# Expert and gate logits of an attention + mixture-of-experts + MLP kernel, computed token by token instead of head pair by head pair

## The chip, the cores and the metric

The kernel runs on one core of a Trainium2 chip. The metric is the device time of one execution in microseconds (us); less is better. Engines are named as the profile names them: PE (TensorE matmul), PEld (TensorE weight load, which overlaps PE), DVE (VectorE), ACT (ScalarE), POOL (GpSimd), SP (SyncE, here only a DMA queue).

## What is computed

Three stages follow each other. Causal attention with a decay for 4 batches of 8 heads of 576 positions and 64 dimensions; a mixture of experts in which each of the 2304 tokens goes to the one expert of 8 with the largest logit; and a dense MLP with a rational activation.

```python
x = attn(q, k, v, f)                      # (4*576 tokens, 8 heads * 64 = 512)
logits = x @ w_gate                       # (2304, 8)
e_idx = argmax(logits, axis=1)
gate_w = softmax(logits)[token, e_idx]
eom = sigmoid(x @ w_output_gate)          # (2304, 8)
for e in range(8):                        # only the rows with e_idx == e
    out[mask] = gate_w * eom[:, e] * (relu(x[mask] @ w1[e]) @ w2[e])
h = out @ w_in
out = P(h) / Q(h) @ w_out
```

The change is in how `x @ w_gate` and `x @ w_output_gate` are made (16 numbers per token in all), and in the short stretch between attention and experts.

## The kernel before, in words

**Attention.** The 32 heads of all batches are worked off as 16 pairs, four pairs to a batch. A pair makes scores on PE (L456, L457, L467, L468, into one of 3 PSUM banks `s`), takes the row minimum on DVE (L479, L491), exponentials on ACT (L511, L522), transposes of the weights on PE (L578, L582, L598, into one of 3 PSUM banks `pt`), copies of these to `pT` on ACT or DVE (L291, L293), and the product with the values on PE (L621, into one of 2 banks `po`). The result of a pair is copied to `ot` (L291 or L293): head dimensions of the two heads on the 128 partitions, the 576 tokens along the row. It isn't yet divided by the softmax's sum.

**The order.** Every step is an `Op` with a wished time and a length for each engine that may do it. `Plan.order` places them greedily on the engines by these numbers and writes each engine's program in that order; engines then work strictly in order, so one that waits holds back all that is behind it. The lengths are the planner's own; the wished times are a table (`T_STEP`, `T_TRANS` and so on).

**A batch.** When a batch's four pairs have `ot`, `batch` adds these steps, in two parts of the tokens (rows 2 to 4 with the 64-row rest first, then rows 0 and 1; a row is 128 tokens). The sums of the two half rows are added (L679), swapped over partitions by a small matmul (L683) and inverted (L697, L698). The logits: for each of the four pairs a matmul with the small weights `wl` (128 partitions, 32 columns: 16 for either head) as the stationary operand and `ot` as the moving one, each pair to its own 32 partitions of one bank `s` (L706); ACT copies the bank to `lgs` (L712); PE transposes `lgs` to token-major, 128 tokens to a matmul, into a bank `pt` (L720); DVE multiplies by the inverted sums (L727) and adds up the 8 heads (L731). Then `choose` (L748 on) picks the expert, `gates_a`, `gates_x` (two exponentials on ACT, L764 and L765) and `gates_b` make the factor `rg`, and the token rows are transposed (`rows_t`, L788), multiplied by `rg` (`rows_m` on DVE, L794; `rows_a` on ACT, L817, eight instructions of 64 columns a row) and stored to `x_d` (`rows_d`, L821).

**The last batch.** Three rows of the last batch but one are held back ("late rows"): their transposes wait for the last batch's logits (`last_tr`), and ACT multiplies them. For the last batch itself everything after the logits is written out by hand behind the planned part: `choose`, two matmuls that count tokens per expert (L954, L956), the transposes of its five rows in a given order, the gates, the counting interleaved on DVE, the rows' products (`rows_out`: rows 0 to 2 on ACT, rows 3 and 4 on DVE, in the order 0 to 4), their stores in the same order on SP's queue, and on DVE the positions that give `ids`, the list of token numbers by expert (L1026).

**The experts' start.** POOL gathers the rows of `x_d` by `ids` (L1164). PE meanwhile runs `warm(20)`, twenty matmuls of no use (L1274), then transposes the first gathered rows (L1183), ACT and DVE split them (`colAh`, `colAl`), and the first expert's matmuls (L1189 to L1191) begin.

Of the kernel before, what the change touches and what calls it, by code (L numbers as in the profile page):

```python
# [15 lines left out]
AF = mybir.ActivationFunctionType  # L16
# [5 lines left out]
P = 128  # L22
# [115 lines left out]
def tile_attention_moe_mlp(  # L138
# [16 lines left out]
    nc = tc.nc  # L155
    B, NHP, D, _ = qT.shape
    H = 2 * NHP
    NBH, S = f.shape
    NT, DM = out.shape
# [60 lines left out]
    with ExitStack() as actx, ExitStack() as rctx:  # L220
# [59 lines left out]
        def wt(tag, shape=(P, S)):  # L280
            return wk.tile(list(shape), F32, tag=tag, name=tag, bufs=plan.buffers.get(tag, 2))
# [4 lines left out]
        def bank(pool, tag):  # L286
            return pool.tile([P, 512], F32, tag=tag, name=tag)
# [73 lines left out]
        def pair(p):  # L361
# [248 lines left out]
            for n, part in enumerate(parts):  # L610
# [21 lines left out]

                def out_t(e, x=x, base=base, end=end):
                    if "ot" not in d:
                        d["ot"] = otp.tile([P, S], F32, tag="ot", name="ot")
                    evac(e, d["ot"][:, base:end], x["po"][:, : end - base])
# [6 lines left out]
        def batch(b):  # L643
# [8 lines left out]
            def wn():  # L652
                cnt[0] += 1
                return TB + cnt[0] * dB

            def make(e):
                for t, shape in (("rc", (P, NI, H)), ("rg", (P, NI, H)), ("lgs", (P, S)), ("lgb", (P, NI, 16)),
                                 ("lmax", (P, NI)), ("sc", (P, NI, NE + 1)), ("den", (P, NI)), ("smax", (P, NI)),
                                 ("ex", (P, NI, NE)), ("gs", (P, NI, NE)), ("oz", (P, NI)), ("tt", (P, NHP))):
                    g[t] = wt(t, shape)  # L660
                nc.gpsimd.memset(g["lgb"], 0.0)

                nc.gpsimd.memset(g["sc"][:, :, NE:], 0.5)
# [6 lines left out]
            prev_red = []  # L670
            for n, part in enumerate(parts):
# [5 lines left out]
                if i1 == NI:  # L677
# [13 lines left out]
                    a2 = plan.op(wn(), {"PE": 30}, swap, [a], takes=["pt"], shape=2)  # L691
# [9 lines left out]
                x = {}  # L701

                def logit(e, x=x, c0=c0, c1=c1):
                    x["ps"] = bank(ps_s, "s")
                    for n_ in range(NHP):
                        nc.tensor.matmul(  # L706
                            x["ps"][32 * n_ : 32 * n_ + 32, : c1 - c0], wl[:, n_, :], ps_[n_]["ot"][:, c0:c1],
                            start=True, stop=True,
                        )

                o_lg = plan.op(wn(), {"PE": (c1 - c0) * 4 / 2.4 + 150}, logit, ready, takes=["s"], shape=3)
                o_cp = plan.op(wn(), {"ACT": 50 + 0.836 * (c1 - c0)}, lambda e, x=x, c0=c0, c1=c1: nc.scalar.activation(  # L712
                    g["lgs"][:, c0:c1], x["ps"][:, : c1 - c0], AF.Copy), [o_lg, o_mk], frees=[("s", o_lg)])
                for r0, r1, np_ in ((i0, full, P),) + (((NQ, NI, TL),) if i1 == NI else ()):
                    y = {}

                    def tr(e, y=y, r0=r0, r1=r1, np_=np_):
                        y["pt"] = bank(ps_t, "pt")
                        for i in range(r0, r1):
                            nc.tensor.transpose(  # L720
                                y["pt"][:np_, (i - r0) * P : (i - r0 + 1) * P], g["lgs"][:, i * P : i * P + np_], identf
                            )
# [12 lines left out]
                    o_tr = plan.op(wn(), {"PE": 109 * (r1 - r0)}, tr, [o_cp, o_n], takes=["pt"])  # L735
# [159 lines left out]
        def rows_out(i):  # L895
            (rows_a if i < 3 else rows_m)(i, last_y[i], wt("pr" if i < 3 else "t")[:, :DM])
            rows_d(i, last_y[i], nc.sync)
# [59 lines left out]
        for i in (3, 4, 0, 1, 2):  # L957
            rows_turn(i)
# [39 lines left out]
        for i in range(NI):  # L998
            rows_out(i)
# [63 lines left out]
    with ExitStack() as ectx:  # L1063
# [214 lines left out]
        warm(20)  # L1278
# [251 lines left out]
```

## Time and profile before

| what | value |
|---|---|
| median of 3 runs | 910.52 us (909.38 to 911.69) |
| profiled execution, its own time | 911.47 us |
| profiled execution, span of the trace | 909.8 us |
| PE busy | 868.8 us, 95% of the span |
| DVE busy | 738.7 us, 81% |
| ACT busy | 623.2 us, 69% |
| POOL busy | 331.8 us, 36% |
| mean granted TensorE clock | 0.986 of full |

The profiled execution takes 1.67 us beside its span, and its own time is 0.95 us over the median. Attention fills the trace from 0 to about 195 us, the passage to the experts 195 to 218.5 us, the experts and the MLP the rest. Busy shares of the whole say little here: what matters is which engine is waited for in each of these three stretches. Matmuls are pipelined, so that the time that PE spends on one is read from the distance of starts, not from its duration.

### The profile page before, as it was taken

The page shows a single profiled execution, that of the slowest core. Times are in us where ns is not written, and L with a number is a line of the kernel's source. Part 1 is how long each engine was busy: PE and PEld are TensorE (multiplying, and loading weights), DVE is VectorE, ACT ScalarE, POOL GpSimd, SP SyncE. Part 2 cuts the span into 40 slices and gives each one's busy share as a digit, 9 for nine tenths or more (in the row PEclk, how much of TensorE's full clock was granted, in tenths as well). Part 3 has the DMA queues.
Part 4 walks back from the last instruction along what each step waited for, and adds up shares of the span by engine and source line. Part 5 has one row for each costly group of instructions (what it writes and reads, how often), then busy time and mean ns, then how long its engine had stood idle before and what let it go on. Part 6 is the DMA issues. An engine that isn't in the chain of part 4 may idle for free. (4 is left out here: it accounts for less than half of the span.)

```text
span 909.8 us, 14910 instructions
## 1 busy us (share of the span) xinstructions
PE 868.8 (95%) x4743; PEld 722.7 (79%) x4743; DVE 738.7 (81%) x1394; ACT 623.2 (69%) x1300; POOL 331.8 (36%) x349
## 2 busy tenths in 40 slices
PE   6999998986999999999999999999999999999996
PEld 5787786765788888788887788899888889988885
DVE  7798999677875689788854899989898888989873
ACT  4889887776564577566633887877676667777664
POOL 7888595502212223123130223243233324224223
PEclk9999999997999999999999999999999999999998
DMA  6676568415764378788642311011000001000001
GB/s 168 159 202 162 155 175 220 150 53 185 261 225 158 131 276 302 253 269 291 227 149 108 123 64 58 1 47 36 12 35 13 24 1 47 24 1 36 1 1 46
DMA packets 50147, 110.25 MB, mean 121 GB/s; under 512 B 8405, under 2 KB 12526, under 8 KB 50062
## 3 DMA queue, kind: packets, MB, share of 16 engines
q1 hardware_dynamic: 39214, 74.09, 26.6%
q0 software_dynamic: 10848, 35.14, 11.4%
q8 instruction: 39, 0.64, 0.3%
q14 instruction: 46, 0.38, 0.1%
HBM read 151.79 MB, written 20.35 MB: 189 GB/s over the span
## 5 line engine op out<-in xcount | busy, mean ns | idle before, releaser
L1429 POOL TENSOR_TENSOR gl<-raw,gh 128x512 fp32r<-128x512 f32 (+1 forms) x80 | 95.8, 1200 | 243.0 <-ACT gh L1428 150.0
L1445 PE MATMUL pa<-wu,gl 128*128 128x512 f32 x288 | 113.1, 393 | 1.1 <-POOL gl L1429 1.1
L1443 PE MATMUL pa<-wu,gh 128*128 128x512 f32 x288 | 113.6, 395 | 0.0
L1444 PE MATMUL pa<-wu,gh 128*128 128x512 f32 x288 | 112.6, 391 | 0.0
L1408 ACT ACTIVATE raw<-ph 128x512 f32<-128x512 f32 (+1 forms) x80 | 44.3, 554 | 79.4 <-PE ph L1400 76.1
L1083 DVE TENSOR_TENSOR colAl<-px,colAh 128x512 fp32r<-128x512 f32 x70 | 47.9, 687 | 46.7 <-ACTq L1094 25.7
L1056 DVE TENSOR_TENSOR wu<-raw,wu 128x1024 fp32r<-128x1024 f32 x64 | 75.4, 1220 | 8.9 <-ACT wu L1054 8.5
L511 ACT ACTIVATE pr<-t,mn 128x384 f32<-128x384 f32 (+3 forms) x128 | 70.7, 556 | 16.3 <-DVE mn L479 15.7
L1411 DVE SCALAR_TENSOR_TENSOR raw<-raw,babs 128x512 f32<-128x512 f32 (+1 forms) x80 | 60.9, 761 | 24.4 <-ACT raw L1409 23.9
L1421 DVE SCALAR_TENSOR_TENSOR raw<-raw,coef,raw 128x512 f32<-128x512 f32 (+1 forms) x80 | 65.9, 824 | 17.4 <-ACT raw L1417 14.2
L1398 PE MATMUL ph<-colAh,wi 128*128 128x512 f32 x192 | 74.9, 390 | 0.8 <-ACTq L1339 0.8
L1399 PE MATMUL ph<-colAl,wi 128*128 128x512 f32 x192 | 74.8, 390 | 0.2 <-DVEq L1339 0.2
L1400 PE MATMUL ph<-colAh,wi 128*128 128x512 f32 x192 | 74.7, 389 | 0.0
L1189 PE MATMUL ph<-wu,colAh 128*128 128x512 f32 x176 | 73.6, 418 | 0.7 <-ACT colAh L1082 0.7
L1189 PE MATMUL py<-wu,colAh 128*128 128x512 f32 x176 | 70.7, 402 | 1.0 <-ACT colAh L1082 1.0
L1191 PE MATMUL ph<-wu,colAl 128*128 128x512 f32 x176 | 69.7, 396 | 0.0
L1190 PE MATMUL ph<-wu,colAh 128*128 128x512 f32 x176 | 69.3, 394 | 0.0
L1191 PE MATMUL py<-wu,colAl 128*128 128x512 f32 x176 | 69.2, 393 | 0.1
L1190 PE MATMUL py<-wu,colAh 128*128 128x512 f32 x176 | 68.6, 390 | 0.0
L1054 ACT ACTIVATE wu<-raw 128x1024 fp32r<-128x1024 f32 x64 | 64.0, 1076 | 4.5 <-DMA raw<-in_w_dram 3.4
L1445 PEld LDWEIGHTS pa<-wu,gl 128*128 128x128 f32 x288 | 54.0, 188 | 13.9 <-POOL gl L1429 2.4
L479 DVE CUSTOM_DVE_ANT_0 t<-s,mask 128x384 f32<-128x384 f32 (+3 forms) x128 | 57.7, 484 | 6.6 <-PE s L457 3.7
(232 smaller groups left out, 2409.0 us busy)
## 6 DMA issues: line engine op xcount, KB each, us to landing
raw<-in_w_dram SPq DMA_DIRECT2D x92, 1024.0 KB
rk<-in_kT_dram SPq DMA_DIRECT2D x30, 288.0 KB
rq<-in_qT_dram SPq DMA_DIRECT2D x30, 288.0 KB
d<-in_w_in_dram POOLq DMA_DIRECT2D x16, 512.0 KB
d<-in_w_out_dram POOLq DMA_DIRECT2D x16, 512.0 KB
y_d<-ys SPq DMA_DIRECT2D x22, 256.0 KB
v<-in_v_dram SPq DMA_DIRECT2D x16, 256.0 KB
wo_d<-d SPq DMA_DIRECT2D x16, 256.0 KB
```

Of the source, the lines that this page charges most:

```text
L511: nc.scalar.activation(u["pr"][:, sl], u["t"][:, sl], AF.Exp, bias=u["mn"][:, m : m + 1], scale=-1.0, accum_out=sm[:, i, 2 * hp + h : 2 * ...
L1056: nc.vector.tensor_tensor(w[:, 1], r, w[:, 0].bitcast(F32), ALU.subtract)
L1189: nc.tensor.matmul(ps, hi[:, c, :], w[:, 0, c, :], start=start and c == 0, stop=False)
L1190: nc.tensor.matmul(ps, hi[:, c, :], w[:, 1, c, :], start=False, stop=False)
L1191: nc.tensor.matmul(ps, lo[:, c, :], w[:, 0, c, :], start=False, stop=stop and c == KD - 1)
L1398: nc.tensor.matmul(out_, wh, hi[:, :, c], start=(c == 0), stop=False)
L1399: nc.tensor.matmul(out_, wh, lo[:, :, c], start=False, stop=False)
L1400: nc.tensor.matmul(out_, wl_, hi[:, :, c], start=False, stop=(c == KD - 1))
L1429: nc.gpsimd.tensor_tensor(d["gl"], d["u_"], d["gh"].bitcast(F32), ALU.subtract)
L1443: nc.tensor.matmul(a_, gh[:, sl], wh, start=(m == 0), stop=False)
L1444: nc.tensor.matmul(a_, gh[:, sl], wl_, start=False, stop=False)
L1445: nc.tensor.matmul(a_, gl[:, sl], wh, start=False, stop=(m == MF - 1))
```

## The change

Logits. The stationary and the moving operand are exchanged: for every row of 128 tokens and every pair, `ot` of these tokens (128 partitions, 128 columns, 64 in the rest) is the stationary operand and `wl` (32 columns) the moving one. The result is token-major at once, in a bank `pt`, and the copy to `lgs` and its transposes are gone, with the tile `lgs` and the bank `s`. The planner's length for it is 100 ns a matmul.

The swap of the half rows' sums waits, in the last batch, for the last pair's first product with the values (`o_pv`), and the logits wait for the swap (`turned`).

By hand: the last batch's rows are transposed in the order 3, 4, 2, 0, 1; row 2 is multiplied on DVE instead of ACT; products and stores go in the order 3, 0, 4, 2, 1; and `warm` has 24 matmuls.

```diff
@@ pair
+                d["o_pv"] = first
@@ batch
-            prev_red = []
+            prev_red, turned = [], []
...
-                    a2 = plan.op(wn(), {"PE": 30}, swap, [a], takes=["pt"], shape=2)
+                    a2 = plan.op(wn(), {"PE": 30}, swap, [a, ps_[-1]["o_pv"] if sums_done else None], takes=["pt"], shape=2)
+                    turned.append(a2)
...
-                def logit(e, x=x, c0=c0, c1=c1):
-                    x["ps"] = bank(ps_s, "s")
-                    for n_ in range(NHP):
-                        nc.tensor.matmul(
-                            x["ps"][32 * n_ : 32 * n_ + 32, : c1 - c0], wl[:, n_, :], ps_[n_]["ot"][:, c0:c1],
-                            start=True, stop=True,
-                        )
-
-                o_lg = plan.op(wn(), {"PE": (c1 - c0) * 4 / 2.4 + 150}, logit, ready, takes=["s"], shape=3)
-                o_cp = plan.op(wn(), {"ACT": 50 + 0.836 * (c1 - c0)}, lambda e, x=x, c0=c0, c1=c1: nc.scalar.activation(
-                    g["lgs"][:, c0:c1], x["ps"][:, : c1 - c0], AF.Copy), [o_lg, o_mk], frees=[("s", o_lg)])
                 for r0, r1, np_ in ((i0, full, P),) + (((NQ, NI, TL),) if i1 == NI else ()):
...
-                    def tr(e, y=y, r0=r0, r1=r1, np_=np_):
+                    def logit(e, y=y, r0=r0, r1=r1, np_=np_):
                         y["pt"] = bank(ps_t, "pt")
                         for i in range(r0, r1):
-                            nc.tensor.transpose(
-                                y["pt"][:np_, (i - r0) * P : (i - r0 + 1) * P], g["lgs"][:, i * P : i * P + np_], identf
-                            )
+                            for n_ in range(NHP):
+                                c = (i - r0) * P + 32 * n_
+                                nc.tensor.matmul(
+                                    y["pt"][:np_, c : c + 32], ps_[n_]["ot"][:, i * P : i * P + np_], wl[:, n_, :],
+                                    start=True, stop=True,
+                                )
...
-                    o_tr = plan.op(wn(), {"PE": 109 * (r1 - r0)}, tr, [o_cp, o_n], takes=["pt"])
+                    o_tr = plan.op(wn(), {"PE": 100 * NHP * (r1 - r0)}, logit, ready + turned, takes=["pt"])
@@ by hand, behind the plan
-            (rows_a if i < 3 else rows_m)(i, last_y[i], wt("pr" if i < 3 else "t")[:, :DM])
+            (rows_a if i < 2 else rows_m)(i, last_y[i], wt("pr" if i < 3 else "t")[:, :DM])
...
-        for i in (3, 4, 0, 1, 2):
+        for i in (3, 4, 2, 0, 1):
             rows_turn(i)
...
-        for i in range(NI):
+        for i in (3, 0, 4, 2, 1):
             rows_out(i)
...
-        warm(20)
+        warm(24)
```

Since the planner sees other steps with other lengths, every engine's order differs from the end of the first batch to the end of attention; before it and from the experts on the instructions stand as they stood. In the rows below L706 and L720 are the logits and the transposes of `lgs`, L713 the new logits, L683 and L685 the swap, L788 and L782 transposes of token rows.

PE at the end of the first batch, behind the values' product of the pair after it (minus is the kernel before, plus the changed one):

```order
 L621 MATMUL po<-pT,v_130 64x256 x2
 L621 MATMUL po<-pT,v_130 64x128 x2
-L683 MATMUL pt<-tt,identf 64x4
-L706 MATMUL s<-ot,wl 32x320 x4
-L706 MATMUL s<-ot,wl 32x256 x4
+L685 MATMUL pt<-tt,identf 64x4
+L713 MATMUL pt<-wl,ot 128x32 x8
 L578 MATMUL pt<-identf,pr 128x128 x4
 L582 MATMUL pt<-identf,pr 128x128
-L720 MATMUL pt<-identf,lgs 128x128 x2
 L456 MATMUL s<-kh,qs_113 128x384
 L457 MATMUL s<-kl_119,q2s_117 128x384
```

Eight small matmuls stand where eight wide ones stood; twelve more follow in two pieces among the next pair's scores, and five transposes are gone.

PE at the end of attention, the kernel before, from the last pair's transposes to the late rows:

```order
L598 MATMUL pt<-identf,pr 128x128 x10
L683 MATMUL pt<-tt,identf 64x4
L621 MATMUL po<-pT,v_129 64x320 x6
L621 MATMUL po<-pT,v_129 64x192 x2
L621 MATMUL po<-pT,v_129 64x64 x2
L621 MATMUL po<-pT,v_129 64x256 x2
L621 MATMUL po<-pT,v_129 64x128 x2
L706 MATMUL s<-ot,wl 32x320 x4
L706 MATMUL s<-ot,wl 32x256 x4
L720 MATMUL pt<-identf,lgs 128x128 x2
L720 MATMUL pt<-identf,lgs 64x128
L720 MATMUL pt<-identf,lgs 128x128 x2
```

The same stretch of the changed kernel:

```order
L598 MATMUL pt<-identf,pr 128x128 x10
L621 MATMUL po<-pT,v_129 64x320 x6
L621 MATMUL po<-pT,v_129 64x192 x2
L621 MATMUL po<-pT,v_129 64x64 x2
L621 MATMUL po<-pT,v_129 64x256 x2
L621 MATMUL po<-pT,v_129 64x128 x2
L685 MATMUL pt<-tt,identf 64x4
L713 MATMUL pt<-wl,ot 128x32 x8
L713 MATMUL pt<-wl,ot 64x32 x4
L713 MATMUL pt<-wl,ot 128x32 x8
L782 MATMUL pt<-identf,ot 128x128 x8
L782 MATMUL pt<-identf,ot 64x128 x4
```

The swap moved from ahead of the last values' product to behind it; 20 small matmuls stand between that product and the late rows' transposes (L782), where 8 wide ones and 5 transposes stood.

SP's queue, the stores of the last batch's five rows before (`pr` is a row made on ACT, `t` one made on DVE):

```order
L821 DMA x_d_68<-pr_3267 128x512
L821 DMA x_d_68<-pr_3277 128x512
L821 DMA x_d_68<-pr_3287 128x512
L821 DMA x_d_68<-t_3297 128x512
L821 DMA x_d_68<-t_3300 64x512
```

And in the changed kernel, where `pr_3291` is row 2, now made on DVE:

```order
L815 DMA x_d_68<-t_3275 128x512
L815 DMA x_d_68<-pr_3278 128x512
L815 DMA x_d_68<-t_3288 64x512
L815 DMA x_d_68<-pr_3291 128x512
L815 DMA x_d_68<-pr_3294 128x512
```

The two rows that DVE makes early no longer stand behind the three of ACT; the last store is that of ACT's second row instead of a row of DVE behind ACT's third.

## Rows read from the trace of the kernel before

**Rows 1.** Stretches: us, PE, PEld, DVE, ACT, POOL busy (count), clock, DMA share, GB/s

```profile
73.00:191.00 118.00, 109.42 (x908) 88.12 (x904) 103.56 (x351) 98.00 (x313) 72.16 (x74) 1.00 0.58 162
...
222.00:900.00 678.00, 673.15 (x3196) 564.64 (x3195) 552.57 (x791) 449.11 (x763) 188.05 (x178) 1.00 0.32 109
```

**Rows 2.** Waits of PE from 76 to 191 us: total, times, longest

```profile
PE s L467 <- DVE mn L479: 4.8, 2, 2.6
```

**Rows 3.** PE in time order behind the first batch: start, us, what, count

```profile
73.25 1.18 PE L706 MATMUL s<-ot,wl 128*32 128x320 f32 x16
74.36 0.66 PE L578 MATMUL pt<-identf,pr 128*128 128x128 f32 x4
...
76.54 1.31 PE L598 MATMUL pt<-identf,pr 128*128 128x128 f32 x10 [0.37 <-DVE tmp L727]
```

**Rows 4.** Weight loads by shape, whole span: count | busy us, mean ns

```profile
L1398 PEld LDWEIGHTS ph<-colAh,wi 128*128 128x128 f32 x192 | 36.1, 188 | 8.7 <-ACTq L1339 1.0 <-PE ph L1400 0.3
...
L706 PEld LDWEIGHTS s<-ot,wl 128*32 128x32 f32 x64 | 1.7, 109 | 1.3 <-issue 0.2
...
L683 PEld LDWEIGHTS pt<-tt,identf 128*64 128x64 f32 x8 | 0.9, 136 | 1.2 <-ACT pT L291 1.2
```

**Rows 5.** Weight loads in time order, two of 128 columns behind each other

```profile
75.08 0.19 PEld L456 LDWEIGHTS s<-kh,qs 128*128 128x128 f32 x1
75.19 0.19 PEld L457 LDWEIGHTS s<-kl,q2s 128*128 128x128 f32 x1
```

**Rows 6.** Weight loads in time order, five for matmuls of 25 moving columns

```profile
208.59 0.21 PEld L1024 LDWEIGHTS <-op__3313 128*128 128x128 f16 x5 [3.66 <-DVE op__3313 L1019]
```

**Rows 7.** End of attention, all engines in time order

```profile
190.26 0.90 ACT L291 ACTIVATE pT<-pt 128x512 f32<-128x512 f32 x2
...
191.79 0.19 PE L683 MATMUL pt<-tt,identf 128*64 128x4 f32 x1 [1.04 <-DVE sums L697]
...
194.73 1.18 PE L706 MATMUL s<-ot,wl 128*32 128x320 f32 x16
...
196.06 0.81 PE L720 MATMUL pt<-identf,lgs 128*128 128x128 f32 x5 [0.15 <-ACT lgs L712]
196.53 0.42 DVE L727 TENSOR_TENSOR tmp<-pt,rc 128x256 f32<-128x256 f32 x1 [3.20 <-PE pt L720]
...
197.01 0.66 PE L788 MATMUL pt<-identf,ot 128*128 128x128 f32 x4
...
197.71 4.90 ACT L817 ACTIVATE xr<-pt,rg 128x64 f32<-128x64 f32 x24 [1.32 <-PE pt L788]
...
199.63 0.20 DVE L748 TENSOR_REDUCE lmax<-lgb 128x5 f32<-128x40 f32 x1
...
202.42 0.30 ACT L764 ACTIVATE ex<-ex 128x40 f32<-128x40 f32 x1
```

**Rows 8.** The passage to the experts, all engines in time order

```profile
204.46 0.68 DVE L794 TENSOR_TENSOR t<-po,rg 128x512 f32<-128x512 f32 x1
...
209.43 0.96 SPq L821 DMA_DIRECT2D x_d<-t  x2
...
211.14 0.18 DVE L1026 TENSOR_SCALAR ids<-pid 128x25 int32<-128x25 f32 x1 [0.41 <-PE pid L1024]
...
213.34 1.44 POOL L1164 DMA_INDIRECT xg<-x_d,ids  x1 [20.72 <-ACT wu L1054]
...
217.14 0.63 PE L1183 MATMUL px<-identf,xg 128*128 128x128 f32 x4 [1.89 <-DMA xg<-x_d,ids]
...
218.51 0.80 PE L1189 MATMUL ph<-wu,colAh 128*128 128x512 f32 x1 [0.75 <-ACT colAh L1082]
```

**Rows 9.** The first expert's matmuls in time order, and PE's stretches (clock third from the end)

```profile
221.97 0.40 PE L1191 MATMUL ph<-wu,colAl 128*128 128x512 f32 x1
222.20 0.40 PE L1189 MATMUL ph<-wu,colAh 128*128 128x512 f32 x1
...
219.50:220.50 1.00, 1.00 (x4) 0.50 0.69 213
```

More of the change, by code (lines that the diff above doesn't have):

```diff
@@ L656, in make @@
             def make(e):
-                for t, shape in (("rc", (P, NI, H)), ("rg", (P, NI, H)), ("lgs", (P, S)), ("lgb", (P, NI, 16)),
+                for t, shape in (("rc", (P, NI, H)), ("rg", (P, NI, H)), ("lgb", (P, NI, 16)),
                                  ("lmax", (P, NI)), ("sc", (P, NI, NE + 1)), ("den", (P, NI)), ("smax", (P, NI)),
@@ L700, in batch @@
                 o_n = plan.op(wn(), {"DVE": 250 * (2 if i1 == NI else 1)}, norm, need + (sums_done or ready) + [o_mk])
-                x = {}
-                def logit(e, x=x, c0=c0, c1=c1):
-                    x["ps"] = bank(ps_s, "s")
-                    for n_ in range(NHP):
-                        nc.tensor.matmul(
-                            x["ps"][32 * n_ : 32 * n_ + 32, : c1 - c0], wl[:, n_, :], ps_[n_]["ot"][:, c0:c1],
-                            start=True, stop=True,
-                        )
-                o_lg = plan.op(wn(), {"PE": (c1 - c0) * 4 / 2.4 + 150}, logit, ready, takes=["s"], shape=3)
-                o_cp = plan.op(wn(), {"ACT": 50 + 0.836 * (c1 - c0)}, lambda e, x=x, c0=c0, c1=c1: nc.scalar.activation(
-                    g["lgs"][:, c0:c1], x["ps"][:, : c1 - c0], AF.Copy), [o_lg, o_mk], frees=[("s", o_lg)])
                 for r0, r1, np_ in ((i0, full, P),) + (((NQ, NI, TL),) if i1 == NI else ()):
                     y = {}
-                    def tr(e, y=y, r0=r0, r1=r1, np_=np_):
+                    def logit(e, y=y, r0=r0, r1=r1, np_=np_):
                         y["pt"] = bank(ps_t, "pt")
                         for i in range(r0, r1):
-                            nc.tensor.transpose(
-                                y["pt"][:np_, (i - r0) * P : (i - r0 + 1) * P], g["lgs"][:, i * P : i * P + np_], identf
-                            )
+                            for n_ in range(NHP):
[4 more added lines that the diff above has]
+                                )
                     def scale(e, y=y, r0=r0, r1=r1, np_=np_):
```

## The prediction

> **What bounds the kernel now.** I read the stretches first, then the waits of the bounding engine, then the chain of instructions where no engine is full. Behind 222 us PE is busy for 673 of 678 us [rows 1]: whatever happens earlier shifts this block as a whole, and the change doesn't touch it. From 73 us, the end of the first batch, to 191 us PE is busy for 109.4 of 118 us, DVE for 103.6, ACT for 98 [rows 1]. So PE bounds attention too, but with 8.6 us of waits, of which 4.8 us in two pieces are for DVE's row minima [rows 2]: DVE is a close second. From 191 to 218.5 us no engine is full; a chain sets the time, and I follow it by its instructions [rows 7, 8]. The prediction is the sum of three shifts: of attention's end, of the start of the first expert's matmuls against that, and of the speed at which these begin.
>
> **Logits on PE, first three batches.** Before: the eight wide matmuls take 1.11 us, from 73.25 to the next start at 74.36, and ten transposes in a row 1.31 us, so five take some 0.60 us [rows 3]. Together 1.71 us a batch.
>
> After: 20 matmuls a batch, 16 with 128 and 4 with 64 stationary columns. An fp32 matmul that is no transpose leaves two load and multiply pairs in the trace: 8 wide matmuls in the order, 16 in the trace [rows 3]. So there are 32 pairs with 128 columns to load and 8 with 64. What does a pair cost? The load is what grew: 32 columns take 109 ns, 64 take 136, 128 take 188 [rows 4]. These lie on a line of 0.82 ns a column over a fixed 83 ns that is pipeline, so 128 columns occupy the loader for 0.105 us; and where two such loads follow each other, they start 0.11 us apart [rows 5]. The multiply has only 32 columns (by the 0.12 us of a transpose of 128, some 0.03 us) and fits under the next load. I take 0.11 us, and 0.055 us for 64 columns: 32 x 0.11 + 8 x 0.055 = 3.96 us, or 2.25 us more a batch and 6.75 us in three. That the form of rows 4 with 128 columns isn't the very one used here (its 188 ns belong to another matrix type) leaves bounds: if load and multiply don't overlap, 0.14 us a pair and 3.4 us more a batch; if the loads go as those for 25 moving columns of another type, five in 0.21 us or 0.042 us each [rows 6], 40 x 0.042 = 1.68 us and no loss. The nearer rows are 4 and 5, of four bytes an element.
>
> How much of the 6.75 us do PE's waits swallow? Between nothing and all, since there are 8.6 us of them. PE makes the scores that DVE works on, so a late PE mostly delays DVE as well, and a wait far behind comes as late again; but DVE and ACT had 14.4 and 20 us to spare [rows 1], and the planner gives DVE two copies fewer. I take 2.0 us as swallowed: **+4.75 us** at attention's end.
>
> The copy of the logits leaves ACT (about 0.8 us a batch); ACT had the 20 us, so it is worth nothing by itself. The logits now hold a bank `pt` instead of `s`; PE is in order and issues nothing else while they run, so this costs nothing beside the time counted.
>
> **The last batch.** Here the logits are on the chain. (a) The swap stood ahead of the last values' product and made PE wait 1.04 us for DVE, until 191.79, while the last copies of `pT` ended at 191.16 [rows 7]. Behind the product it waits for nothing. The gain is between 0 and 0.6 us; with some 0.3 us for the signal I take 0.35. (b) The logits then begin at 194.73 - 0.35 = 194.38, and the pieces end at 196.14, 196.58 and 198.34. DVE's first product came 0.25 us behind the second transpose (started 196.06, 0.11 us long, next 196.53) [rows 7], so now at 196.4; its third piece, for the last logits, at 198.6. With 0.42 us and the sum of the heads `choose` begins at 199.7 instead of 199.63: no gain. (c) Queued behind the logits on PE are the late rows' transposes: 198.34 instead of 197.01, **1.33 us later**. ACT waits for them, multiplies for 4.90 us, and only then comes to the two exponentials of the gates, which DVE, behind them the factors `rg`, all products and `ids` wait for [rows 7]. So the gates come at 203.75 instead of 202.42.
>
> (d) Row 2 on DVE: one more product of 0.68 us, of which 0.65 on DVE's way to `ids`: 211.14 + 1.33 + 0.65 = 213.12. (e) The gather. It started at 213.34, two us behind `ids`, because the last stores went out only at 209.43, behind ACT's third row [rows 8]. The new last store is behind ACT's second row: one row is a third of 4.90 us, so it goes out some 1.6 us earlier in the chain, and with the 1.33 us still before the old time. So `ids`, ready at 213.3, becomes what the gather waits for. No row shows the gather behind `ids` alone: the lag is between 0 and the 2.0 us of before; I take 0.8, gather at 214.1, **0.75 us later**, and with it the transposes and the first expert's matmuls (218.51).
>
> (f) The clock. From the first expert's first matmul at 218.51 to its ninth at 221.97 PE took 3.46 us, at a granted clock of 0.50 (the lower level, 1.2 GHz), where at full clock they start 0.23 us apart, 1.9 us for eight distances [rows 8, 9]: 1.6 us lost. Ahead of it PE was idle for 1.89 us between `warm` and the gathered rows [rows 8]. Now `warm` starts 2.0 us later with `ids`, the rows come 0.75 us later, so 0.64 us of the gap are left, and four more matmuls fill most of it. Between 0 and 1.6 us; I take **-1.5 us**, since the cause, an idle PE ahead, all but goes.
>
> **Sum.** +4.75 + 0.75 - 1.5 = +4.0 us. From the profiled execution's own 911.47 us that gives 915.5; its place over the median being chance, from the median of 910.52 it is **914.5 us**.
>
> **Rivals.** *The small matmuls are cheap.* If a pair costs 0.042 us [rows 6], the three batches lose nothing. The last batch's chunk takes 1.68 us, the late rows start at 196.06, 0.95 us earlier, `ids` at 211.14 - 0.95 + 0.65 = 210.84, the gather 0.8 us behind its end at 211.8, 1.5 us earlier; with the clock -3.0 us: 907.5 us. It decides at 0.043 us a pair for attention; for the sum to be zero, the pair may cost about 0.07 us. For it: matmuls of few columns do go that fast in this trace. Against it: the line of rows 4. Chance 0.2.
>
> A page of the Trainium skill would have it so: TensorEngine Tiling (Array Packing), Performance Considerations, Instruction Overhead, puts every matmul of up to 60 columns at the same 60 cycles, by which forty pairs would take 1.0 us at 2.4 GHz, less than before, and the time would be near 906 us, an estimate from that page. The same section (When to Use Tiling) speaks against the change all the same: with a moving side of 32 columns it advises to swap the operands and tile the columns, which is the form that is given up. Only that second sentence agrees with rows 4.
>
> *PE's waits swallow it.* If DVE, not PE, sets the pace of attention, the 6.75 us fit into the 8.6 us of waits, and what is left is the passage, +0.75 - 1.5: 909.8 us; half swallowed, 912.5. For it: DVE is busy 88% of the stretch. Against it: PE is busy 93%, and its waits are in few places. Chance 0.22, all within the noise.
>
> *Worse than forecast.* Without overlap, 0.14 us a pair: three batches +10 us, less 2, the chunk 1.2 us longer, gather and experts likewise: about 920 us. An order made with 0.8 us for what takes 1.8 us adds waits of DVE for the logits. Chance 0.1. That the change doesn't do what it says, a new wait for banks in place of the copy, would show in the same places, and is in these cases.
>
> **How the numbers follow.** A difference of 0.3% (2.7 us) is about what can be told from none: 907.8 and 913.3 us. Forecast, 913.3 to 919: 0.48. Worse: 0.1. Swallowed: 0.22. Cheap: 0.2, of which a good half is below 907.8, the rest within. Slower 0.58, same 0.25, faster 0.17. The range is 907.0 to 920.0: below it lies a part of the cheap case, above it one of the worse.
>
> **What would show it.** Right: the new logits' loads of 128 columns last near 188 ns and start 0.11 us apart; eight of them take 1.8 us; between 73 us and the last product PE is busier by some 6 us; the late rows' transposes start over a microsecond later behind the last product; the gather follows `ids` within a microsecond; the first expert's matmuls start 0.23 us apart. Wrong: loads 0.05 us apart or less (cheap), PE's waits shrunk to 2 us or less with DVE nearly full (swallowed), or matmuls still 0.43 us apart behind the gather (no clock gain, +1.5 us).

## Result and profile after

The changed kernel takes 920.86 us (median of 4 runs, 919.75 to 923.0), the kernel before 909.95 in the same comparison: 1.0106 times as long, 95% interval 1.0087 to 1.0125, or some 9.6 us more. The forecast was 914.5 us with a range up to 920.0: the direction was right, the amount less than half of it, and the time lies 0.9 us above the range. The profiled execution took 919.75 us, with a span of 918.0 us, 8.2 more than before; times within one trace below are from it.

From the first expert on the work is the same (behind 222 us PE is busy for 673 of 678 us here too, as in [rows 1]). The extra time is in attention. I measure it from the start of the first batch's logits to the start of the last product with the values, which holds the same work in every kernel below but for the logits and the last swap. First the kernel before, then the changed one, and in it the stretch around the second batch's logits (columns as in [rows 1]: PE busy is the first number behind the comma, the clock the third from the end):

```profile
73.25:191.75 118.50, 109.17 (x904) 87.88 (x900) 104.29 (x353) 97.91 (x312) 72.66 (x75) 1.00 0.57 160
```

```profile
73.51:200.00 126.49, 119.90 (x961) 99.88 (x957) 104.06 (x355) 98.06 (x305) 73.71 (x75) 0.97 0.55 155
117.10:123.90 6.80, 5.59 (x28) 4.86 (x27) 4.99 (x17) 3.32 (x11) 1.14 (x2) 0.50 0.00 0
```

Attention takes 8.0 us more: PE is busy for 10.7 us more and idle for 2.7 us less (6.6 instead of 9.3). And for 6.8 us the granted clock is 0.50, the lower of its two levels (1.2 GHz), where before it was 1.00 throughout. PE in time order just ahead of that, and PE's waits from 76 to 201 us, which answer to [rows 2]:

```profile
113.09 0.34 PE L457 MATMUL s<-kl,q2s 128*128 128x384 f32 x1
114.46 1.97 PE L713 MATMUL pt<-wl,ot 128*128 128x32 f32 x16 [1.03 <-ACT pT L291]
116.27 0.38 PE L467 MATMUL s<-kh,qs 128*128 128x288 f32 x1
...
119.11 0.69 PE L598 MATMUL pt<-identf,pr 128*128 128x128 f32 x2 [1.21 <-ACT pr L511]
```

```profile
PE s L467 <- DVE mn L479: 1.8, 2, 1.1
PE pt L598 <- ACT pr L511: 1.6, 2, 1.2
PE pt L713 <- ACT pT L291: 1.0, 1, 1.0
PE pt L782 <- DVE ot L293: 0.8, 1, 0.8
```

The waits for the row minima fell from 4.8 us [rows 2] to 1.8, but new ones came: the logits wait for a bank `pt`, and transposes behind them wait for the exponentials. The price of the logits, answering to [rows 3, 4]: 16 pairs of load and multiply from 73.51 to 75.32 us, 0.113 us each, and the loads by shape:

```profile
73.51 1.97 PE L713 MATMUL pt<-wl,ot 128*128 128x32 f32 x16
75.32 0.31 PE L578 MATMUL pt<-identf,pr 128*128 128x128 f32 x1
```

```profile
L713 PEld LDWEIGHTS pt<-wl,ot 128*128 128x128 f32 x128 | 14.9, 192 | 1.6 <-ACT pT L291 1.4 <-issue 0.2
L713 PEld LDWEIGHTS pt<-wl,ot 128*64 128x64 f32 x32 | 2.5, 158 | 1.0 <-DVE tmp L721 0.4 <-DVE lgb L725 0.4 <-DVE pT L293 0.2
```

The passage, all engines in time order, answering to [rows 7, 8, 9]:

```profile
200.06 3.02 PE L621 MATMUL po<-pT,v 128*64 128x320 f32 x26
...
203.23 4.46 PE L713 MATMUL pt<-wl,ot 128*128 128x32 f32 x40
...
207.52 1.51 PE L782 MATMUL pt<-identf,ot 128*128 128x128 f32 x12
...
208.19 4.91 ACT L811 ACTIVATE xr<-pt,rg 128x64 f32<-128x64 f32 x24 [4.47 <-PE pt L782]
208.80 0.20 DVE L742 TENSOR_REDUCE lmax<-lgb 128x5 f32<-128x40 f32 x1
...
212.91 0.31 ACT L758 ACTIVATE ex<-ex 128x40 f32<-128x40 f32 x1
...
222.23 0.18 DVE L1020 TENSOR_SCALAR ids<-pid 128x25 int32<-128x25 f32 x1 [0.40 <-PE pid L1018]
...
223.27 1.53 POOL L1158 DMA_INDIRECT xg<-x_d,ids  x1 [29.40 <-DVE ids L1020]
...
227.28 0.63 PE L1177 MATMUL px<-identf,xg 128*128 128x128 f32 x4 [0.41 <-DMA xg<-x_d,ids]
...
228.66 0.50 PE L1183 MATMUL ph<-wu,colAh 128*128 128x512 f32 x1 [0.74 <-ACT colAh L1076]
...
230.87 0.39 PE L1185 MATMUL ph<-wu,colAl 128*128 128x512 f32 x1
```

The first expert's matmuls start 28.60 us behind the last product, before 26.71 (218.51 less 191.80 in [rows 7, 8]). The clock is at full speed for them at once: they take 2.21 us from the first to the ninth, against 3.46 before [rows 8, 9].

### The profile page after: what moved, and what is told of

Read it like the earlier page. It is cut to its first block, busy times and chain, and to the rows that moved or that the text cites. A ratio compares the mean times of both kernels' runs of the same rounds, so it can differ in the third digit from the quotient of the medians.

```text
span 918.0 us, 15057 instructions
## 1 busy us (share of the span) xinstructions
PE 880.2 (96%) x4823; PEld 736.1 (80%) x4823; DVE 737.6 (80%) x1395; ACT 621.5 (68%) x1284; POOL 331.9 (36%) x349
```

## Experiments

The table has one row a kernel, from its profiled execution: attention as defined above with what PE is busy and idle in it, the time at a clock of 0.50 in it, the distance from the last product's start to the first expert's first matmul ("passage"), and the ratio of times to the kernel before. All in us but the last. The kernel before took 911.7 to 912.3 us beside these kernels, so ratios are compared, not times.

| kernel | attention | PE busy | idle | at 0.50 | passage | time / before (95%) |
|---|---|---|---|---|---|---|
| before | 118.5 | 109.2 | 9.3 | 0 | 26.7 | 1 |
| changed | 126.5 | 119.9 | 6.6 | 6.8 | 28.6 | 1.0106 (1.0087 to 1.0125) |
| new_first | 127.2 | 120.0 | 7.1 | 6.8 | 26.7 | 1.0079 (1.0061 to 1.0097) |
| new_last | 117.2 | 109.1 | 8.1 | 0 | 29.6 | 1.0002 (0.9991 to 1.0013) |
| rows_only | 119.0 | 109.4 | 9.6 | 0 | 26.4 | 0.9986 (0.9971 to 1.0000) |
| rows_swap | 117.7 | 109.3 | 8.4 | 0 | 26.7 | 0.9978 (0.9963 to 0.9993) |
| plan220 | 118.9 | 116.7 | 2.2 | 0 | 29.3 | 1.0014 (1.0001 to 1.0027) |
| first220 | 118.7 | 116.5 | 2.2 | 0 | 26.4 | 0.9985 (0.9971 to 0.9999) |
| plan280 | 120.6 | 115.1 | 5.5 | 0 | 29.1 | 1.0049 (1.0031 to 1.0068) |
| plan_b1 | 126.0 | 118.1 | 7.9 | 6.8 | 28.4 | 1.0083 (1.0063 to 1.0102) |
| plan_notb1 | 124.9 | 118.3 | 6.6 | 3.4 | 29.1 | 1.0062 (1.0038 to 1.0085) |
| rows_len1_5 | 121.5 | 113.5 | 8.0 | 3.4 | 26.3 | 1.0033 (1.0011 to 1.0054) |
| rows_len0_5 | 125.1 | 115.0 | 10.1 | 3.4 | 26.3 | 1.0041 (1.0027 to 1.0056) |
| wide | 125.5 | 118.9 | 6.6 | 0 | 29.1 | 1.0098 (1.0079 to 1.0117) |
| wide2 | 125.0 | 117.8 | 7.2 | 0 | 28.7 | 1.0089 (1.0069 to 1.0109) |
| double | 142.1 | 137.2 | 4.9 | 17.1 | 29.9 | 1.0270 (1.0245 to 1.0296) |
| double_wide2 | 134.5 | 129.2 | 5.3 | 0 | 28.7 | 1.0186 (1.0159 to 1.0213) |

### Which part of the change costs: new_first, new_last, rows_only, rows_swap

`new_last` has the old logits in batches 0 to 2 and the new ones in the last; `new_first` the reverse; `rows_only` is the kernel before with the by-hand rows of the change; `rows_swap` adds to that the late swap.

```diff
@@ new_last (new_first has b == B - 1)
+                OLD = b < B - 1
+                if OLD:
...
@@ rows_swap, against rows_only
-                    a2 = plan.op(wn(), {"PE": 30}, swap, [a], takes=["pt"], shape=2)
+                    a2 = plan.op(wn(), {"PE": 30}, swap, [a, ps_[-1]["o_pv"] if sums_done else None], takes=["pt"], shape=2)
```

> The changed kernel, with the old logits (wide matmuls, copy by ACT, transpositions) in the first three batches and the new ones in the last batch alone; the rows by hand stay as changed (order 3, 4, 2, 0, 1; row 2 on DVE; stores 3, 0, 4, 2, 1; 24 matmuls of warming). Theory A: attention up to the last product of PE ends within 0.6 us of the kernel before (191.8 us); the passage has the new logits' 4.3 us on the chain and costs 1.9 us up to the first expert's first matmul, the clock behind it gives 1.9 us back: 910 us, within 1.5 us of the kernel before. Rival (the passage is where the time went): 915 us or more. Rival (the planner's order changed everywhere): the last product ends 2 us or more later although no small matmul stands in the first three batches.

> The changed kernel, with the new logits in the first three batches and the old ones (wide matmuls, copy by ACT, transpositions) in the last; the rows by hand stay as changed. Theory A: the last product of PE starts about 8 us later than before (6.75 us of pairs and up to 3.4 us of clock, less 2 us of waits taken up); the passage then is that of the kernel before with the changed rows, 0 to 0.6 us longer up to the first expert's matmuls, and the clock gives 1.9 us back: 916 to 917 us. Without a drop of the clock it is 913 us. Rival (the passage is where the time went): 912 us or less.

> The kernel before with the by-hand part of the change alone: rows transposed in the order 3, 4, 2, 0, 1, row 2 multiplied on DVE, products and stores in the order 3, 0, 4, 2, 1, 24 matmuls of warming. The logits and the swap are those of before, so attention ends as before (last product at 191.8 us). Theory A: the changed kernel's passage lost 1.9 us up to the first expert's first matmul by late rows that came 2.25 us later; without that delay the gather comes 0.5 to 1.5 us earlier than before relative to the last product, the idle PE ahead of the first expert's matmuls shrinks below 1 us, and these start at full clock (0.23 us apart instead of 0.43): 1.5 to 3 us less than before, 907 to 908.5 us by a median before of 910. Rival: the rows' order gains nothing by itself, since ids, not the stores, are what the gather waits for, and the clock stays low for the first matmuls: within 1 us of the kernel before.

> The old logits with the by-hand rows of the change (910.5 us), and of the changed kernel's new conditions that of the swap alone: the last batch's swap of the half rows' sums stands behind the last product with the values instead of ahead of it, the only difference in PE's order. Step (a) of the prediction: PE's wait of 1.04 us for the sums goes, and the product starts when the last copies of pT are there: 0.35 us earlier in the passage (0 to 0.6). Rival: the swap's result comes later and the copies into the sums with it, so the first products of the logits wait on DVE: no gain, or 0.5 us more.

Measured: `new_last` 1.0002 (its passage 2.9 us longer, where 1.9 was expected), `new_first` 1.0079, `rows_only` 0.9986, `rows_swap` 0.9978 of the time before. `new_first` and `new_last` have the late swap too, so each is compared with `rows_swap`. At 912 us, the new logits of the first three batches cost 1.01% or 9.2 us (`new_first`), those of the last batch 0.24% or 2.2 us (`new_last`); the rows by hand with their longer warming give 0.14%, 1.3 us, back (the interval reaches to 1.0000), and the late swap 0.08%, 0.7 us (intervals overlap). Together that is 9.4 of the 9.6 us. The last batch's price stands in the passage column: 29.6 against 26.7 us, 2.9 us; the trace of `new_last` has the forty pairs of the last batch from 192.96 to 197.25 us, 4.3 us, with ACT's late rows behind them.

The rows' gain is smaller than I expected, and their trace shows where a part of it goes: the first expert's matmuls start at full clock, but PE then waits, and the clock falls later instead.

```profile
230.97 0.50 PE L1189 MATMUL py<-wu,colAh 128*128 128x512 f32 x1 [1.65 <-ACT colAh L1082]
```

```profile
218.80:222.50 3.70, 3.70 (x17) 2.81 (x18) 2.32 (x15) 0.37 (x1) 1.82 (x3) 1.00 0.78 218
...
232.50:235.90 3.40, 3.40 (x10) 2.52 (x9) 3.22 (x6) 0.60 (x1) 0.00 (x0) 0.52 0.84 277
```

The late swap takes 1.36 us off attention (119.03 to 117.67) and the passage becomes 0.36 longer, so 1.0 us by the traces, 0.7 by the ratios. PE in `rows_swap`, where nothing is waited for ahead of the last product any more:

```profile
190.55 1.77 PE L598 MATMUL pt<-identf,pr 128*128 128x128 f32 x10
192.26 3.24 PE L621 MATMUL po<-pT,v 128*64 128x320 f32 x26
```

```profile
74.59:192.26 117.67, 109.32 (x905) 87.92 (x901) 103.21 (x351) 97.42 (x311) 71.59 (x74) 1.00 0.61 162
```

### The planner's length: plan220, plan280, plan_b1, plan_notb1

Only the number by which the planner reckons a small matmul is altered; instructions are the same and PE's order differs in 36 to 94 rows, taken away and put in together, of some 750 in attention.

```diff
-                    o_tr = plan.op(wn(), {"PE": 100 * NHP * (r1 - r0)}, logit, ready + turned, takes=["pt"])
+                    o_tr = plan.op(wn(), {"PE": 220 * NHP * (r1 - r0)}, logit, ready + turned, takes=["pt"])
@@ plan280: 280.  plan_b1: (220 if b == 1 else 100).  plan_notb1: (100 if b == 1 else 220)
```

> The changed kernel with one number of the planner altered: it reckons 220 ns for a small matmul of the logits (what it takes in the trace, 1.81 us for eight) instead of 100. Instructions are the same, their order on the engines another. Theory A (the loss in attention is the work of the pairs and the clock behind them): PE between 73 us and its last product stays busy for 120 us, and the time stays within 2 us of 920.86, with the dip of the clock where short waits still stand beside the small matmuls. Rival B (the planner's wrong length brings the waits beside the small matmuls, and these the clock): waits of PE of 6.6 us shrink by 1.5 us or more, the clock stays at 1.00, and the time is 915 to 918 us.

> The changed kernel with 280 ns for a small matmul in the planner, more than the 0.226 us it takes. Batch 1's matmuls stand behind the product as with 220 ns (rows 515 and 522 of PE's order); 82 rows of PE's order differ from those with 220 ns. Theory P (the place): within 2 us of the kernel with 220 ns, 911.5 to 915 us, clock 1.00 from 73 to 190 us. Rival L (the length has to be right): 916 us or more.

> The changed kernel, the planner's length of a small matmul 220 ns for the second batch (batch 1) alone and 100 ns for the others. On PE batch 1's first eight matmuls keep the place they have in the changed kernel (row 486 of PE's order, ahead of the pair's second half of scores, where they waited 1.03 us for a bank in the changed kernel and the clock fell behind them), while steps behind them move. Theory P (the place of batch 1's logits in PE's order makes the waits and the drop of the clock, not the length as such): the wait of 1 us ahead of them and the clock of 0.50 at about 117 us come again; last product of PE at 198 us or later, time 917 to 921 us. Rival L (a planner that knows the length makes a good order): the last product by 194 us, time 912 to 915 us.

> The changed kernel, the planner's length of a small matmul 100 ns for the second batch (batch 1) and 220 ns for the others: the other half of the pair with 220 ns in batch 1 alone. Batch 1's first twelve small matmuls stand at row 515 of PE's order, behind the next product with the values, as in the kernel with 220 ns everywhere (913.2 us), though their length is wrong. Theory P (the place): no wait of 1 us ahead of them, clock 1.00 from 73 to 190 us, last product at 192.5 to 194 us, time 912 to 914.5 us. Rival L (the length): the time of the changed kernel, 918 us or more.

`plan220`: 1.0014, so that most of the loss, 8 us, is gone with the same work. My theory A of then is refuted, and rival B holds (the time came out under its 915 to 918 us). PE is busy for 7.5 us more than in the kernel before, and idle for 7.1 us less (1.2 of these by the swap, as `rows_swap` against `rows_only` shows): its waits are all but filled.

```profile
73.83:192.70 118.87, 116.67 (x961) 97.85 (x957) 99.43 (x353) 98.69 (x305) 74.31 (x75) 1.00 0.59 164
```

```profile
117.22 2.93 PE L621 MATMUL po<-pT,v 128*64 128x320 f32 x28
119.97 0.23 PE L685 MATMUL pt<-tt,identf 128*64 128x4 f32 x2
120.13 2.55 PE L713 MATMUL pt<-wl,ot 128*128 128x32 f32 x24
122.61 0.44 PE L456 MATMUL s<-kh,qs 128*128 128x384 f32 x1
```

```profile
PE s L467 <- DVE mn L479: 1.4, 2, 0.7
PE pt L598 <- ACT pr L511: 0.7, 2, 0.5
```

The second batch's logits stand behind a product with the values here and wait for nothing; in the changed kernel they stood ahead of half the next scores and waited for a bank. (24 pairs take 2.48 us; with the 16 that follow, 1.71 us, a batch costs 4.19 us.)

`plan_b1` keeps them at the bad place, with their right length; wait and clock come again, 1.0083, as the place theory says:

```profile
113.14 1.97 PE L713 MATMUL pt<-wl,ot 128*128 128x32 f32 x16 [1.02 <-ACT pT L291]
117.76 0.47 PE L598 MATMUL pt<-identf,pr 128*128 128x128 f32 x1 [2.65 <-ACT pr L511]
```

`plan_notb1` has them at the good place with the wrong length, and I expected 912 to 914.5 us. It took 917.4 (1.0062), between the theories and nearer to rival L's 918. The second batch is clean, but another wait of 2.53 us came at 160 us, in the third, with the clock at 0.50 from 160.84 us on:

```profile
159.98 0.71 PE L598 MATMUL pt<-identf,pr 128*128 128x128 f32 x2 [2.53 <-ACT pr L511]
```

`plan280` took 916.3 us, above the 911.5 to 915 of the place theory: no drop of the clock, but 5.5 us of waits. So that one place isn't the cause as such: a small change of a length deals all waits anew, and the time goes with PE's waits and the clock in the order that results. Whether the right length brings a good order (rival L) stays open. Its number for `plan280`, 916 us or more, came, and the best of the five orders is the one with the right length throughout; `plan_b1`, which has it in one batch only, speaks against it. One order for each length can't tell a rule from luck.

### Two separate terms: first220

`new_first` with 220 ns.

> New logits in the first three batches, planned with 220 ns a small matmul; the old logits (wide matmuls, copy, transpositions) in the last batch; rows by hand as changed. With 220 ns and new logits everywhere the last product came at 192.73 us and the first expert's first matmul 29.3 us behind it; with the old logits in the last batch that distance was 26.4 to 26.7 us. If attention and passage are two separate terms, the last product comes at 192 to 194 us, the distance is 26.2 to 27.0 us, and the time is 2 to 3 us below the 913.2 us of the kernel with 220 ns, 910 to 911.5 us. Rival: the passage isn't separate (the clock or the late rows behind another attention make it longer), 912.5 us or more.

0.9985 (909.79 us, a little under the 910 to 911.5 expected): attention 118.7, passage 26.4, as the two terms add up. Against `rows_swap` (0.9978), which has the late swap too, the new logits of three batches then cost 0.6 us, with overlapping intervals: 7.3 us more of PE's work, 6.1 us fewer waits.

### The control: order alone, with the old logits

> A control: the old logits (with the by-hand rows of the change, which alone took 910.5 us), with nothing altered but the planner's length of the wide logits, one and a half times as long. The work on every engine is the same, 184 rows of PE's order differ. Theory O (the order alone moves attention's end by microseconds, up or down, through PE's waits): the last product moves by 2 us or more from 192.4 us, with PE's waits of 9.8 us ahead of it moved by the same. Rival W (it's the work that counts; the order moves little): within 1 us of 910.5 us.

> The same control with the planner's length of the wide logits halved; 236 rows of PE's order differ, the work is the same. Theory O (the order alone moves attention's end by microseconds): the last product moves by 2 us or more from 192.4 us, with PE's waits ahead of it moved by the same, and not in the same amount as in the other control. Rival W: within 1 us of 910.5 us.

```diff
-                o_lg = plan.op(wn(), {"PE": (c1 - c0) * 4 / 2.4 + 150}, logit, ready, takes=["s"], shape=3)
+                o_lg = plan.op(wn(), {"PE": 1.5 * ((c1 - c0) * 4 / 2.4 + 150)}, logit, ready, takes=["s"], shape=3)
```

Against `rows_only`'s 0.9986 they take 1.0033 and 1.0041, 4.3 and 5.0 us more, with no work added: rival W falls. First the last product's start in each of the two, then attention in `rows_only` and in them:

```profile
193.62 0.48 PE L621 MATMUL po<-pT,v 128*64 128x320 f32 x1
198.49 0.48 PE L621 MATMUL po<-pT,v 128*64 128x320 f32 x1
```

```profile
73.35:192.38 119.03, 109.41 (x906) 87.95 (x902) 104.35 (x354) 97.95 (x312) 72.71 (x75) 1.00 0.58 160
72.08:193.62 121.54, 113.54 (x906) 90.93 (x902) 106.84 (x356) 98.49 (x310) 71.42 (x74) 0.99 0.54 156
73.36:198.49 125.13, 114.99 (x905) 91.72 (x901) 107.70 (x355) 98.63 (x311) 71.75 (x74) 0.99 0.54 152
```

Attention is 2.5 and 6.1 us longer, and the passage, 26.3 us, is that of `rows_only`: the order alone moves attention by microseconds. The mechanism that I had named doesn't hold: PE's waits are 1.6 us fewer in the first and 0.5 us more in the second. Instead PE is busy for 4.1 and 5.6 us more with the same instructions. Both have a clock of 0.50 for 3.4 us (behind waits of 4.06 and 2.24 us), which at half speed is 1.7 us at most; where the rest goes stays open.

### The clock: wide, wide2, double, double_wide2

`wide` gives each small matmul 128 moving columns (`wl` four times over; the surplus is overwritten or not read); `wide2` does so for the matmuls of 128 loaded columns only. `double` issues the small matmuls of three batches twice; `double_wide2` is both.

```diff
@@ wide
-                                    y["pt"][:np_, c : c + 32], ps_[n_]["ot"][:, i * P : i * P + np_], wl[:, n_, :],
+                                    y["pt"][:np_, c : c + P].rearrange("p (t c) -> p t c", c=32),
+                                    ps_[n_]["ot"][:, i * P : i * P + np_],
+                                    wl[:, n_, :].unsqueeze(1).to_broadcast([P, 4, 32]),
@@ double
-                        for i in range(r0, r1):
+                        for i in [i for i in range(r0, r1) for _ in range(2 if b < B - 1 else 1)]:
```

> The changed kernel (920.86 us), with each small matmul of the logits given 128 moving columns instead of 32: wl four times over, read with a stride of zero; the 96 columns beyond the 32 are overwritten by the next matmul or never read. Loads, order of all engines and result are the same. In the changed kernel the granted clock fell to 0.50 from 117 to 124 us, right behind eight of the small matmuls (114.46 to 116.27 us) that had an idle PE of 1.03 us ahead of them. Theory A: a pair is bound by its load (0.113 us in the changed kernel's trace), and the multiply of 32 columns leaves TensorE's array with little to do; with 128 columns a pair still takes 0.11 to 0.12 us, the clock stays at 1.00 from 73 to 200 us, and the time falls by the 3.4 us lost there, to about 917.5 us. Rival B: the clock fell for PE's waits, which stay as they are: the clock falls again in the same place, 920 to 921 us. Rival C: the multiply is not hidden under the load: a pair takes 0.14 to 0.17 us, eight matmuls 2.3 us or more instead of 1.81, and the time rises by 3 us or more.

> The changed kernel with the small matmuls of the first three batches issued twice in the same place (row by row, the second time with the same result); the order of all else is unchanged, and the planner doesn't know of it. It adds 32 pairs of 0.113 us and 8 of 0.058 us a batch, 12.2 us of PE's work in three. Theory A (PE bounds, its waits swallow about a quarter): the last product 9 to 12.2 us later than in the changed kernel, time 930 to 933 us. Rival S (the pairs are swallowed where PE waits, and it was something else that made the changed kernel slow): 6 us more or less, 927 us at most. A pair at another price shows in the distance of the starts: 16 pairs in 1.81 us, 32 in 3.6 us.

> As the earlier kernel with 128 moving columns, but for the matmuls of 128 loaded columns alone; those of 64 keep 32 moving columns. In the earlier kernel eight matmuls of 64 loaded columns came to 1.02 us instead of 0.5, which took 1.5 us of what the clock gave. Theory C (the drop of the clock in attention comes from the small multiplies; with 128 columns the clock stays, at the same price of a pair): clock 1.00 from 73 to 190 us, last product 2 us or more ahead of the changed kernel's 200.06 us, time 916 to 918.5 us on the scale of 920.9 for the changed kernel. Rival W (the drop comes from PE's waits, and what it costs is taken up by the next wait): 920 us or more.

> As the kernel with the small matmuls of the first three batches issued twice (938.15 us; granted clock 0.50 in four stretches of 3.4 to 6.8 us each between 85 and 201 us), with 128 moving columns for those of 128 loaded columns. Same order, same loads. Theory C (the small multiplies bring the clock down): no stretch at 0.50 from 73 to 190 us, the last product 5 us or more ahead of 215.16 us, time 930 to 934 us. Rival W (the clock falls whatever the multiplies' width, for PE's waits): the same stretches at 0.50, 937 us or more.

`wide` kept the clock at 1.00 through attention, as its theory A has it (theory C from `wide2` on), but the time stayed at 1.0098 instead of falling to 917.5 us: its matmuls of 64 loaded columns became dearer, 0.109 us apart instead of 0.058, and took part of the gain back. `wide2` (1.0089) left these as they were:

```profile
70.87:195.84 124.97, 117.81 (x962) 97.80 (x958) 104.48 (x355) 98.28 (x305) 73.79 (x75) 1.00 0.56 157
```

Its attention is 1.6 us shorter than the changed kernel's, and its PE 2.1 us less busy; by the ratios the drop is worth 1.5 us, with intervals that overlap, and the time misses the 916 to 918.5 us expected (1.0089 is 919.3 on that scale). The 1.5 us are less than the 3.4 us by which a stretch of 6.8 us at half speed is longer: PE was busy for only 5.6 us of it, and part of that gain probably goes into other waits (7.2 us instead of 6.6).

The doubled pair of kernels settles what brings the clock down here. `double` has four stretches at 0.50, the first in a place where PE waited for nothing; first PE in time order, then the same time by stretches:

```profile
82.10 4.14 PE L713 MATMUL pt<-wl,ot 128*128 128x32 f32 x32
86.05 0.67 PE L598 MATMUL pt<-identf,pr 128*128 128x128 f32 x2
```

```profile
82.10:85.10 3.00, 3.00 (x30) 3.00 (x28) 0.77 (x4) 1.69 (x6) 0.00 (x0) 1.00 0.14 44
85.10:88.50 3.40, 3.40 (x18) 3.40 (x18) 2.02 (x8) 0.49 (x1) 0.00 (x0) 0.50 0.00 0
```

`double_wide2`, the same loads in the same order with wider multiplies, has none in attention, and is 7.7 us faster by the ratios (1.0270 and 1.0186, intervals apart):

```profile
82.55 3.73 PE L718 MATMUL pt<-wl,ot 128*128 128x128 f32 x32
```

```profile
73.47:207.95 134.48, 129.22 (x1081) 110.00 (x1077) 105.04 (x355) 98.28 (x305) 73.86 (x75) 1.00 0.53 145
```

So theory C holds: a run of small multiplies behind full loads can bring the clock down, without any wait. It need not: an equal run earlier in `double`, and those of the first three batches in `plan220`, left it at 1.00.

```profile
73.07:76.66 3.59, 3.59 (x36) 3.59 (x33) 2.45 (x7) 1.75 (x6) 3.35 (x4) 1.00 1.00 271
```

It isn't the only way: in `plan_notb1` and `rows_len1_5` it fell behind a plain wait of 2.5 and 4.1 us. That the wait did it isn't shown, since waits of up to 2.6 us left it at 1.00 in the kernel before [rows 1, 2]. Both doubled kernels missed what I expected, `double` since its clock fell for 17 us, `double_wide2` on the other side: doubling costs 9.6 us of attention there (11.4 us more busy, 1.9 less idle), where I had reckoned 12.2 us of work. The price of a pair with 128 loaded columns is the load's: 32 pairs take 3.57 us with 128 moving columns (82.55 to 86.12), 0.112 each, as with 32.

## Where the prediction was right and where it failed

**The price of the logits: right.** Forecast 0.11 us a pair, 3.96 us a batch; measured 0.113 and 4.19 (`plan220`), so 2.48 us more a batch instead of 2.25. The bounds of 0.042 and 0.14 us fall. Why the loads of [rows 6] went so much faster, with 128 columns as well, the traces show only as a difference of type (f16 there, f32 here). The Trainium skill, TensorE: Matmul & The Clock Gate, section Weight-path perf modes, states that a fast weight load applies to 128 weights when the type isn't FP32, and the two durations, 0.042 and 0.113 us, agree. The rival that came with another page of the Trainium skill, TensorEngine Tiling (Array Packing), Instruction Overhead, 60 cycles for a small matmul, is refuted for this form: forty pairs take 4.19 us and not 1.0, since the load, which that rule leaves out, is what PE pays.

**Swallowed by PE's waits, 2.0 us: the step that failed.** In the changed kernel itself the number looks good: 2.7 us fewer waits, of which the swap explains 1.2 (`rows_swap`). But I took the waits of the kernel before as a stock of which work uses up a share. The runs show that they belong to the order, and the drop of the clock with them: with the same instructions PE waited 2.2 us (`plan220`), 5.5 (`plan280`) or 7.9 us (`plan_b1`). The change changes the order everywhere behind the first batch, and by the planner's length of 100 ns for what takes 226 it drew one of the bad ones; 8 us of the loss go with that number alone. I had come near it ("An order made with 0.8 us for what takes 1.8 us adds waits of DVE for the logits"), within a tenth, and with no size; the waits that came are PE's own, for ACT. The order should have carried a spread of several us on both sides: in one order the rival "swallowed" is all but true, and three batches cost 0.6 us.

**The clock in attention: no term for it.** This is the second step that failed. I had treated the clock only where PE idles ahead of the experts. Small multiplies brought it down as well: 2.1 us of PE's time in attention (`wide2`). Sum for attention: forecast +4.75 us, less 0.35 for the swap, 4.4; measured 8.0: busy +10.7 (7.5 for the pairs by `plan220`, 2.1 clock, the rest, 1.1, not told apart), idle -2.7. Of the signs that I had set for the forecast, one came at another size: PE busier by some 6 us, measured 10.7.

**The passage.** (a) The swap: forecast 0.35 us, measured by `rows_swap` some 1.0 in the trace. The last product doesn't wait for all copies of `pT`, as I assumed: it starts 1.7 us behind the first of the last ten transposes (190.55 to 192.26 us). (b) `choose` begins 8.74 us behind the last product's start instead of 7.83, 0.9 later, where the forecast's steps come to 0.4 (0.07 and the swap's 0.35): the forty pairs took 4.3 us, not 3.96, and DVE's third piece waits for the last of them. (c) Late rows 7.46 us behind the product instead of 5.21: 2.25 us later, by the steps of the forecast 1.7 (1.33 and the swap's 0.35); the rest is the pairs' price again and the swap, which now stands between the pieces of the product. (d, e) `ids` come 22.17 us behind the product instead of 19.34, and the gather 0.86 us behind their end, forecast 0.8: what it waits for did change from the stores to `ids`. The first expert's matmuls start 1.9 us later against the product; the forecast's steps come to 1.1. (f) The clock at the experts' start: up at once, as foreseen; 1.25 us gained by the ninth matmul, and about 1.9 in all, since the spans differ by 8.2 us and the starts of the first expert by 10.15.

**The rivals.** "Cheap" is out by the loads. "Worse than forecast" is what came in time, by something near its second mechanism; its first, loads and multiplies that don't overlap, is out. "Swallowed" was all but true for another order. Two slips in the rivals' numbers change nothing here: half of 6.75 us swallowed gives 913.1 us, not 912.5, and the shares of "slower" and "faster" put 0.17 of the 0.2 for "cheap" below 907.8 us, more than "a good half".

The best of the kernels run is `rows_swap`, the old logits with the rows by hand and the late swap: 0.9978 (0.9963 to 0.9993), ahead of both. In the best order that was run, the new logits of the first three batches were free within the intervals; in the last batch they cost over 2 us.

## To carry over

When a planner sets the order, a change of work is also a change of order, and its waits can't be reckoned from those of before: price the work, give the order a spread of its own (here some 8 us for the same instructions), tell the planner what the new step really takes, and measure the order that comes of it (the true length gave the best of five orders here, which may be luck). A small matrix as the moving side made PE pay here for the loads of the large one, 0.112 us each. Before a run of such matmuls is put into a full-clock stretch, look in the trace at what the clock does behind it.

## What the runs showed of the hardware

The granted clock can fall while PE's records show no gap: in `double` it went from 1.00 to 0.50 behind 3.00 us in which 3.00 us were busy with pairs of a load of 128 columns and a multiply of 32; with multiplies of 128 columns, at the same 0.112 us a pair, it stayed at 1.00 (`double_wide2`). Such a run need not do it: 3.59 us of the same pairs earlier in `double` left the clock at 1.00.
